# VectorE makes the constants; the first two visits score in banks 0 to 3; first layers of tiles 0 and 1 by w_in piece and half tile; the written orders are replaced

## The chip, the core and the metric

One NeuronCore of a Trainium2 chip runs the whole program. The metric is the device time of one execution in microseconds (us). The core has TensorE (PE, matrix products into PSUM), VectorE (DVE), ScalarE (ACT), GpSimd (POOL) and SyncE (SP). In this kernel POOL issues all input loads, SP issues the stores and the transposing copies. PSUM has eight banks; the kernel numbers them 0 to 7, and the names at0, at1 (two banks each, later la0 to la3) are banks 0 to 3, mp0 to mp3 banks 4 to 7.

## The reference: what is computed

Sliding-window causal attention, then a two-layer feed-forward network with silu on its output:

```python
# q, k, v: 8 batches x 8 heads x 576 positions x 64, float32
scores = (q @ k.T) / sqrt(64)                 # a query sees itself and the 63 keys before it
attn = softmax(where(0 <= i - j < 64, scores, -1e9)) @ v
x = attn.transpose(0, 2, 1, 3).reshape(4608, 512)
h = x @ w_in                                   # w_in 512 x 2048
out = (h * sigmoid(h)) @ w_out                 # w_out 2048 x 512
```

## The kernel before, in words

**Attention.** The 8 x 9 blocks of 64 queries are taken four at a time: 18 visits, u = 0 to 17, each with all 8 heads. A visit has the steps s (scores, 64 small products with 32-row weights, L391 for u below 5, L378 later), exp (two ACT instructions of 1024 columns, L403), mask, pv (32 products with 64-column weights, L431 or L418), inverse and norm on DVE (L442, L445), and the turn of the result into the layout of the network's input: by PE and a copy (ot L457, bridge L464) for visits 0, 1, 2, 3 and 5, by a transposing DMA on SP otherwise. Visits 0 and 1 have no mask step: a product of the identity with a window matrix puts a large negative number into the banks before the scores are added (bias, L386). In visit 1 bias and scores go to banks 4 to 7 (UP = 4), and its four exp instructions take 512 columns each.

**What feeds a visit.** POOL loads the rows of k and q of a visit (L315), DVE transposes them (turn_blocks, L321), and copies of 32 rows move the preceding key block beside each one (shift_k, L308, on ACT or DVE). The values v come in as pairs of blocks (load_v, L338) and are shifted by 64 partitions (shift_v, L362).

**Network.** 4608 tokens are nine tiles of 512. For tiles 0 to 5 the first layer takes 16 column tiles of w_in (ft) by 4 chunks (c): for one ft four products of 512 columns fill one of banks 4 to 7, and ACT takes silu of it (L472, L477). Tile 0's first six ft are computed in two halves of 256 tokens instead (NF0 = 6), so that they can begin when visit 0 alone is done. The second layer of tile 0 is plain (L540), from tile 1 on a seven-product (Strassen) form is used (L544), and tiles 6 to 8 use it in the first layer too (L502). Some products are issued as two halves of 64 weight columns (expert_mm, L467), next to pv, whose weights have 64 columns.

**What sets the order.** Nothing is scheduled by hand in the main part: class Plan (L18) simulates the engines at build time. Every step is added with a class, a duration per engine, its predecessors and, where needed, a group of PSUM banks; within a class steps keep their order, and whenever an engine is free the class head that is ready and has the lowest rank goes next. The ranks are a table of numbers (L237). Loads are one class, in the order of the string SEQ (L166): k and q of visit 0 (letter a), two loads of v, k and q of visit 1 (b), the constants (i), two loads of v, three pieces of w_in (w), a piece of w_out (o), and so on. A piece of w_in is 256 of the 2048 columns. Eight loads at most are under way (L86). PE fills idle time ahead of the first network product with products of zeros ("warm", L974, 41 of them here). A visit's scores may run only after a number of network products (GO, L158).

**Constants.** POOL makes the identity and the window between the loads (L246, L251), ACT copies half of the window (L258), DVE clears the margins of k and v (L265, L269) and makes the 0/1 mask (L261). A silu of a spare tile after the exps of visit 1 brings the table of silu in early (L985).

## Time and profile before

| what | value |
|---|---|
| runs shown | 280.84, 281.28, 280.3 us; median 280.84 us |
| span of the profiled execution (first to last instruction) | 280.6 us |
| mean granted TensorE clock | 0.994 |
| busy | PE 271.8, DVE 203.7, ACT 175.8, POOL 109.3 us |
| first network product | at 19.29 us |
| last PE instruction done | at about 277.1 us |

The span starts 0.24 us ahead of the first instruction that is counted as busy. The profiled execution has no time of its own on record beside its span of 280.6 us; the median of the three runs lies 0.28 us above that span. A timeline row gives start, duration, engine, line, operation, output and input, count, and in brackets how long the engine had been idle and what released it. A window row gives for each engine the busy time (and the number of instructions) in the order PE, PEld (weight loads), DVE, ACT, POOL, then the granted clock, the mean share of DMA engines that are busy, and GB/s.

### The profile page before, as it was taken

The page shows a single profiled execution, that of the slowest core. Times are in us where ns is not written, and L with a number is a line of the kernel's source. Part 1 is how long each engine was busy: PE and PEld are TensorE (multiplying, and loading weights), DVE is VectorE, ACT ScalarE, POOL GpSimd, SP SyncE. Part 2 cuts the span into 40 slices and gives each one's busy share as a digit, 9 for nine tenths or more (in the row PEclk, how much of TensorE's full clock was granted, in tenths as well). Part 3 has the DMA queues.
Part 4 walks back from the last instruction along what each step waited for, and adds up shares of the span by engine and source line. Part 5 has one row for each costly group of instructions (what it writes and reads, how often), then busy time and mean ns, then how long its engine had stood idle before and what let it go on. Part 6 is the DMA issues. An engine that isn't in the chain of part 4 may idle for free.

```text
span 280.6 us, 8735 instructions
## 1 busy us (share of the span) xinstructions
PE 271.8 (97%) x3704; PEld 197.2 (70%) x3704; DVE 203.7 (73%) x380; ACT 175.8 (63%) x272; POOL 109.3 (39%) x163
## 2 busy tenths in 40 slices
PE   8799999999999999899999999999999999999995
PEld 4367445446876488566885488647888888888884
DVE  4682458999868599789698568947587867868641
ACT  2768884976568683857637675665556664565631
POOL 8976776649787599584680000000000000000000
PEclk9979999999999999999999999999999999999999
DMA  9999999999999999999999602540013001101303
GB/s 85 172 197 187 186 185 185 220 220 143 123 217 164 126 146 153 152 177 139 134 165 189 71 2 77 97 96 0 4 37 112 3 32 67 57 0 40 112 20 132
DMA packets 105863, 32.42 MB, mean 116 GB/s; under 512 B 90464, under 2 KB 104800, under 8 KB 105824
## 3 DMA queue, kind: packets, MB, share of 16 engines
q0 software_dynamic: 82336, 19.02, 84.4%
q1 hardware_dynamic: 23488, 12.85, 22.6%
q8 instruction: 29, 0.48, 0.8%
q14 instruction: 10, 0.08, 0.1%
HBM read 38.01 MB, written 9.44 MB: 169 GB/s over the span
## 4 chain that ended last, share of the span: by engine, by line
PE 83%; DMA 8%; issue 3%; DVE 3%; POOL 2%; ACT 1%; DVEq 0%; POOLq 0%; ACTq 0%
PE mp L470 57%; PE la L509 8%; PE la L470 6%; PE mp L509 5%; DMA vv<-in_v_dram 3%; PE at L374 2%; DMA nat<-in_k_dram 2%; PE at L425 2%; DMA nat<-in_q_dram 2%; PE at L437 1%; POOL vv L345 1%; PE at L461 1%; PE mp L974 1%; POOL nat L316 1%; DVE eo L406 1%
## 5 line engine op out<-in xcount | busy, mean ns | idle before, releaser
L470 PE MATMUL mp<-bridge,w_in_sb 128*128 128x512 bf16 (+3 forms) x521 | 86.7, 367 | 0.2 <-ACT gt L478 0.2
L478 ACT ACTIVATE gt<-mp 128x512 bf16<-128x512 f32 (+1 forms) x102 | 56.6, 573 | 22.0 <-PE mp L470 21.2
L470 PEld LDWEIGHTS <-w_in_sb 128*128 128x128 bf16 (+1 forms) x521 | 41.4, 103 | 38.0 <-issue 0.8
L470 PEld LDWEIGHTS <-gs 128*128 128x128 bf16 x512 | 49.4, 98 | 6.0
L403 ACT ACTIVATE eo<-at 128x1024 bf16<-128x1024 f32 x34 | 34.0, 1027 | 14.0 <-PE at L374 12.7
L470 PEld LDWEIGHTS <-gt 128*128 128x128 bf16 (+1 forms) x422 | 34.1, 102 | 9.5 <-issue 0.4
L470 PE MATMUL mp<-ws,gs 128*128 128x256 bf16 x320 | 40.3, 273 | 0.0
L470 PE MATMUL mp<-w_out_sb,gt 128*128 128x256 bf16 (+3 forms) x278 | 38.6, 310 | 0.0
L345 POOL DMA_DIRECT2D vv<-in_v_dram x38 | 33.6, 898 | 3.0 <-DMA w_out_sb<-in_moe_w_out_dram 1.3
L293 POOL DMA_DIRECT2D nat<-in_q_dram x40 | 24.0, 608 | 17.8 <-DMA vv<-in_v_dram 10.0
L406 DVE TENSOR_TENSOR eo<-eo,mask 128x1024 bf16<-128x1024 bf16 x32 | 21.6, 681 | 6.9 <-ACT eo L403 6.7
L293 POOL DMA_DIRECT2D nat<-in_k_dram x40 | 24.2, 617 | 6.1 <-DMA nat<-in_k_dram 3.0
L909 ACT COPY ot<-mp 128x512 f32<-128x512 f32 (+1 forms) x28 | 15.8, 563 | 15.5 <-PE mp L470 14.4
L520 ACT ACTIVATE eo<-vv 128x512 bf16<-128x512 f32 (+1 forms) x18 | 13.9, 773 | 16.2 <-DVE vv L800 16.2
L445 DVE TENSOR_TENSOR eo<-at,rc 128x512 bf16<-128x512 f32 x36 | 22.9, 674 | 0.2
L533 DVE TENSOR_TENSOR gs<-gt 128x1024 bf16<-128x1024 bf16 x24 | 16.3, 686 | 8.5 <-ACT gt L478 8.5
L912 DVE TENSOR_TENSOR ot<-mp,ot 128x512 f32<-128x512 f32 (+1 forms) x21 | 13.8, 658 | 5.7 <-PE mp L470 4.6
L800 DVE TENSOR_TENSOR vv<-mp,vv 128x512 f32<-128x512 f32 x15 | 10.3, 689 | 7.1 <-PE mp L509 7.1
L509 PEld LDWEIGHTS <-w_in_sb 128*128 128x128 bf16 x144 | 14.1, 98 | 1.6
L800 DVE TENSOR_TENSOR vv<-la,vv 128x512 f32<-128x512 f32 x21 | 13.8, 683 | 2.0 <-PE la L509 1.7
L470 PE MATMUL mp<-w_out_sb,gs 128*128 128x256 bf16 x112 | 14.0, 273 | 0.0
L470 PE MATMUL mp<-ws,gt 128*128 128x256 bf16 (+1 forms) x128 | 11.8, 273 | 0.2 <-DVE ot L912 0.2
(121 smaller groups left out, 384.7 us busy)
## 6 DMA issues: line engine op xcount, KB each, us to landing
out_dram<-ot SPq DMA_DIRECT2D x32, 256.0 KB, 3.3
vv<-in_v_dram POOLq DMA_DIRECT2D x38, 128.0 KB, 6.6
nat<-in_k_dram POOLq DMA_DIRECT2D x40, 72.0 KB, 5.8
nat<-in_q_dram POOLq DMA_DIRECT2D x40, 72.0 KB, 5.5
w_in_sb<-in_moe_w_in_dram POOLq DMA_DIRECT2D x8, 256.0 KB, 8.4
w_out_sb<-in_moe_w_out_dram POOLq DMA_DIRECT2D x8, 256.0 KB, 8.1
out_dram<-ot SPq DMA_DIRECT2D x8, 128.0 KB, 1.8
nat<-in_k_dram POOLq DMA_DIRECT2D x3, 256.0 KB, 6.2
```

What stands on the lines that cost most here:

```text
L293: nc.gpsimd.dma_start(out=nats[i].bitcast(BF16)[32 * r:32 * r + 32].rearrange("s (g y) -> s g y", y=128), in_=(q, k)[kk][b, h].rearrange(" ...
L345: nc.gpsimd.dma_start(out=vv[b % NVB][:, t, :, 0:D], in_=v[b, :, 64 * t - 64:64 * t + 64].rearrange("h s d -> s h d"),)
L403: nc.scalar.activation(out=dst, in_=src, func=ACTF.Exp, scale=scale)
L406: nc.vector.tensor_mul(es[w], es[w], mask)
L445: nc.vector.tensor_mul(oxs[o].rearrange("p x c (r d) -> p x (c r) d", r=2), at_pv(op, hf)[:, :, :, 0:D], rcs[r].unsqueeze(3).to_broadcast( ...
L470: nc.tensor.matmul(o[cols], lhsT=w[:, cols], rhs=x, **kw)
L478: nc.scalar.activation(out=gts[0][:, ft, lo:hi], in_=bank(bk)[:, lo:hi], func=ACTF.Silu)
L509: nc.tensor.matmul(bank(bk)[:, HT * f:HT * f + HT], lhsT=w[:, c, 128 * (2 * u + f):128 * (2 * u + f) + 128], rhs=rhs, start=first and f == ...
L520: nc.scalar.activation(out=gt_of(j)[:, f0:f0 + 2, lo:hi], in_=src, func=ACTF.Silu)
L533: (nc.vector.tensor_sub if i else nc.vector.tensor_add)(sums[i][:, f0:f1], x[:, f0:f1], y[:, f0:f1])
L800: d[k] = p.add("plus", {"DVE": 0.69}, lambda _: nc.vector.tensor_add(o, halves(bk), o), [op] + deps)
L909: return p.add("piece", {"ACT": 0.18 + 0.0008 * n}, lambda e: copies[e](out=flat(o), in_=bank(bk)[:, 0:n]), [end] + deps)
```

## The change

- **Constants on DVE.** POOL's five instructions and ACT's copy are replaced by DVE instructions: a row 0 to 127 by doubling (one memset and seven additions), its transpose as a column, three additions of 32, 64 and 96, the identity by comparing row and column, the window from the square of the distance (three instructions), and a copy of half of it. POOL then issues only loads.
- **Visit 1 in banks 0 to 3.** bias is four steps, one for each bank, and exp of visit 1 is two instructions of 1024 columns, as in visit 0.
- **First layers of tiles 0 and 1** in jobs: one piece of w_in (two ft) by half a tile (256 tokens), eight products of 256 columns into one bank, and one silu for both ft. A job needs one piece and one visit's output.
- **Orders.** For every step of visits 0 to 3, the constants and the jobs of both tiles, a written order for each engine (SCRIPT) replaces the ranks; the loads ahead have a written order of 70 (LOADS); new ranks; the gates count PE time (AFTER) in place of products (GO); WHOLE names 19 stretches of products that are not halved. The spare silu is dropped.

The core of the diff (the long tables are cut to a line or two, and durations given to the planner are left out):

```diff
-    def const_ident(_):
-        nc.gpsimd.memset(ident, 0.0)
-        nc.gpsimd.affine_select(out=ident, in_=ident, compare_op=ALU.not_equal, fill=1.0, ...
+    def const_row(n):
+        if n == 0:
+            nc.vector.memset(row[:, 0:1], 0.0)
+        else:
+            nc.vector.tensor_scalar_add(row[:, n:2 * n], row[:, 0:n], float(n))
+    def const_column(_):
+        nc.vector.transpose(out=column, in_=row[:, 0:32])
+    def const_quarter(r):
+        rows = slice(32 * r, 32 * r + 32)
+        nc.vector.tensor_scalar_add(column[rows, 0:1], column[rows, 0:1], 32.0 * r)
+    def const_ident(_):
+        nc.vector.tensor_scalar(ident, row, column[:, 0:1], None, op0=ALU.is_equal)
+    def const_far(_):
+        nc.vector.tensor_scalar(far, row[:, 0:64], column[:, 0:1], 32.5, op0=ALU.subtract, op1=ALU.add)
+    def const_away(_):
+        nc.vector.tensor_tensor(out=away, in0=far, in1=far, op=ALU.mult)
     def const_window(_):
-        nc.gpsimd.memset(window, 0.0)
-        nc.gpsimd.affine_select(...)
-        nc.gpsimd.affine_select(...)
+        nc.vector.tensor_scalar(window, away, 1024.0, -32768.0, op0=ALU.is_gt, op1=ALU.mult)
     def const_window0(_):
-        nc.scalar.copy(out=window0[64:128], in_=window[64:128])
+        nc.vector.tensor_copy(out=window0[64:128], in_=window[64:128])
...
-    def bias(u):
-        for r in range(4):
-            nc.tensor.matmul(bank_at(UP * u + r), lhsT=ident, ...
+    def bias(u, r):
+        nc.tensor.matmul(bank_at(r), lhsT=ident, ...
     def scores_blocks(u):
-                    o = bank_at(r + (UP if u == 1 else 0))
+                    o = bank_at(r)
...
+    def first_early(op, j, f, h):
+        v0 = 4 * j % NBR + 2 * h
+        for s in range(2):
+            for c in range(NDC):
+                ft = 2 * f + s
+                nc.tensor.matmul(bank(op)[:, HT * s:HT * s + HT], lhsT=w_in_sb[:, c, ft * 128:(ft + 1) * 128],
+                                 rhs=bridge[:, v0:v0 + 2, c], start=(s == 0 and c == 0), stop=(s == 1 and c == NDC - 1),
+                                 skip_group_check=True)
+    def silu_early(bk, f, h):
+        nc.scalar.activation(out=gts[0][:, 2 * f:2 * f + 2, HT * h:HT * h + HT], in_=halves(bk), func=ACTF.Silu)
...
-    p.add("prime", {"ACT": 0.2}, lambda _: nc.scalar.activation(out=spare, in_=zero, func=ACTF.Silu), ...
-            si = (add_first_seven if seven else add_first)(n_tile, pool)
+            si = (add_first_seven if seven else add_first if n_tile > 1 else add_first_early)(n_tile, pool)
-    SEQ = "a v b i v w w w o w w w y w o w c d o o v y o o e o o y".split()
+    SEQ = "a v b v w w w o w w w y w o w c d o o v y o o e o o y".split()
+    LOADS = [0, 1, 4, 3, 2, 6, 7, 5, 17, 14, 10, 8, 13, 19, 9, 20, 22, 21, 23, 28, 12, 24, 11, 27, 18, 26, 15, 25, 16, ...
+        "PE": ( "bias3 bias2 bias0 bias1 s0 pv0 pv1 bias6 ot0 bias7 bias4 ot1 bias5 s1 job6 job5 pv2 pv3 job2 job0 ot3 ot2 job4 job10 "
+            "job8 job7 job9 job13 job14 job12 job15 job3 job1 job11 s2 s3 pv4 ot5 pv5 ot4 ot6 ot7 job20 job16 ...
```

Job n is piece n of w_in with visit 0's tokens for n below 8, and piece n - 8 with visit 1's tokens for 8 to 15.

How the instructions move, at three places. First DVE from the end of the clearing of margins to the turn of visit 0's q. Names: kt holds visit 0's keys, qt its queries, nat a loaded tile; gs is lent to visit 1's keys. Before:

```order
L266 MEMSET vv_84 128x72
L267 MEMSET vv_84 64x8x32
L275 MEMSET window_68 128x64
L276 MEMSET zero 128x4
L958 MEMSET kt_81 32x8x64
L322 STREAM_TRANSPOSE kt_81<-nat_70 128x8x2x32
L313 COPY kt_81<-kt_81 32x8x128
L322 STREAM_TRANSPOSE qt_79<-nat_71 128x8x2x32
```

Now, the last rows of the constants and the same steps:

```order
L303 TENSOR_SCALAR far<-row,column 128x64
L306 TENSOR_TENSOR away<-far 128x64
L338 MEMSET window_70 128x64
L309 TENSOR_SCALAR window<-away 128x64
L1028 MEMSET kt_83 32x8x64
L319 MEMSET vv_84 128x72
L320 MEMSET vv_84 64x8x32
L312 COPY window_70<-window 64x64
L382 STREAM_TRANSPOSE kt_83<-nat_72 128x8x2x32
L300 TENSOR_SCALAR ident<-row,column 128x128
L373 COPY kt_83<-kt_83 32x8x128
L382 STREAM_TRANSPOSE qt_81<-nat_73 128x8x2x32
```

Sixteen new DVE instructions now stand ahead of the first turn and the identity stands right behind it; one small memset has gone and one pair that clears a margin of v stands later.

Second, POOL's queue from its first load. Before:

```order
L316 DMA nat_70<-in_k_dram 128x8x128
L316 DMA nat_71<-in_q_dram 128x8x128
L345 DMA vv_82<-in_v_dram 128x8x64 x2
L316 DMA nat_72<-in_k_dram 128x8x128
L316 DMA nat_73<-in_q_dram 128x8x128
L252 MEMSET window 128x64
L253 ISA
L253 AFFINE_SELECT window<-window 128x64
L255 AFFINE_SELECT window<-window 128x64
L247 MEMSET ident 128x128
L248 AFFINE_SELECT ident<-ident 128x128
L345 DMA vv_82<-in_v_dram 128x8x64 x2
```

Now:

```order
L376 DMA nat_72<-in_k_dram 128x8x128
L376 DMA nat_73<-in_q_dram 128x8x128
L376 DMA nat_74<-in_k_dram 128x8x128
L405 DMA vv_84<-in_v_dram 128x8x64 x4
L376 DMA nat_75<-in_q_dram 128x8x128
L411 DMA w_in_sb<-in_moe_w_in_dram 128x4x256 x7
```

The first eight loads are the same eight; visit 1's q moves from the sixth place to the eighth and its k from the fifth to the third. Behind them the row before has three pieces of w_in, one of w_out, three of w_in and two loads of v; now seven pieces of w_in follow at once.

Third, PE where the network begins ("..." for repeated rows). Before, after the turns of visit 0's output:

```order
L461 MATMUL mp_115<-ident,eo 128x128
...
L437 MATMUL at_112<-vv_82,eo 64x65
...
L470 LDWEIGHTS w_in_sb
L470 MATMUL mp_113<-bridge,w_in_sb 64x256
```

Now, from visit 1's scores:

```order
L456 MATMUL at_114<-qt_81,gs_93 128x64
L541 LDWEIGHTS w_in_sb
L541 MATMUL mp_115<-bridge,w_in_sb 128x256
...
L496 MATMUL at_113<-vv_84,eo 64x65
...
L541 MATMUL mp_118<-bridge,w_in_sb 128x256
```

Before, all pv of visit 1 stood ahead of the first network product; now the first two jobs (16 products) stand between visit 1's scores and its pv.

235 lines of the change are left out of this document (133 added, 102 removed), and 13 rows, old and new, of the table SCRIPT.

## The prediction

> **What bounds the kernel now.** The page first: its span and its line of busy time.
>
> ```profile
> span 280.6 us, 8735 instructions
> PE 271.8 (97%) x3704; PEld 197.2 (70%) x3704; DVE 203.7 (73%) x380; ACT 175.8 (63%) x272; POOL 109.3 (39%) x163
> ```
>
> PE is busy for 97% of the span, so only PE's work, PE's waits and what stands ahead of its first useful product count. Next the windows by stage, which tell where PE is not busy (first number after the length).
>
> ```profile
> 10.00:20.00 10.00, 7.66 (x165) 4.92 (x166) 8.03 (x17) 7.61 (x12) 8.48 (x12) 0.83 1.64 189
> 40.00:60.00 20.00, 19.91 (x254) 10.26 (x254) 17.26 (x30) 15.07 (x23) 11.41 (x18) 1.00 1.52 214
> 80.00:100.00 20.00, 19.85 (x321) 12.30 (x319) 15.14 (x30) 15.67 (x23) 14.88 (x23) 1.00 2.10 162
> 100.00:120.00 20.00, 18.80 (x397) 14.59 (x397) 17.30 (x34) 13.29 (x18) 15.53 (x24) 1.00 1.61 153
> 140.00:160.00 20.00, 19.61 (x276) 12.62 (x262) 15.05 (x34) 11.42 (x18) 6.16 (x8) 1.00 1.42 151
> 264.00:281.00 17.00, 13.11 (x121) 11.51 (x118) 6.02 (x12) 5.17 (x13) 0.00 (x0) 1.00 0.24 78
> ```
>
> From 20 us to the last product PE is idle for 0.09 + 0.15 + 1.20 + 0.39 = 1.83 us; the windows not shown there are full, and the last one holds the end, where the stores finish. What else can be gained lies in the opening and at the end. There busy time misleads, since products of zeros count as work; the timeline tells them apart, and the chain of waits gives PE from 19.45 on.
>
> ```profile
> 5.65 0.71 DVE L322 STREAM_TRANSPOSE kt<-nat 128x512 f32<-128x512 f32 x1 [2.08 <-DMA nat<-in_k_dram]
> 9.32 0.68 PE L397 MATMUL at<-qt,kt 32*128 32x64 bf16 x64
> 9.67 1.04 ACT L367 COPY vv<-vv 64x1024 bf16<-64x1024 bf16 x1 [1.75 <-DMA vv<-in_v_dram]
> 10.73 1.02 ACT L403 ACTIVATE eo<-at 128x1024 bf16<-128x1024 f32 x1
> 11.06 0.71 DVE L322 STREAM_TRANSPOSE gs<-nat 128x512 f32<-128x512 f32 x1 [1.12 <-DMA nat<-in_k_dram]
> 14.61 0.67 PE L397 MATMUL mp<-qt,gs 32*128 32x64 bf16 x62 [0.51 <-DVE gs L313]
> 14.82 0.69 DVE L445 TENSOR_TENSOR eo<-at,rc 128x512 bf16<-128x512 f32 x1
> 16.54 0.50 DVE L365 COPY vv<-vv 64x512 bf16<-64x512 bf16 x1
> 17.41 1.28 ACT L985 ACT_TABLE_LOAD   x1
> 18.41 1.04 PE L437 MATMUL at<-vv,eo 128*64 128x65 bf16 x32
> 19.29 1.25 PE L470 MATMUL mp<-bridge,w_in_sb 128*64 128x256 bf16 x20
> ```
> ```profile
> 20.87 0.66 PE mp L470 x6
> 21.75 12.56 PE mp L470 x74
> 34.31 0.62 PE at L397 x58
> 249.17 0.87 PE mp L470 x8
> ```
>
> The first network product starts at 19.29. By 21.75 visits 0 and 1 are finished and 20 half products and 6 whole ones of 256 columns are done, 16 in all; eight of that size take 0.87 us (last row), so 1.74 us of the first layer. From there to the scores of visit 2 at 34.31 PE has no gap. So the figure to beat is 21.75 - 1.74 = 20.01: the time at which an unbroken first layer would have begun, with both visits' attention out of the way.
>
> **The loads.** The loads go through one queue in order. Asked for a single load each, the views of the eighth load (the second of the two of v that take 1.80 us from 8.04, so issued at about 8.9) and of the first piece of w_in (issued at 9.81) give, from issue to landing:
>
> ```profile
> DMA to landing us min/median/max: 5.3/5.6/5.9
> DMA to landing us min/median/max: 5.7/5.7/5.7
> 8.04 1.80 POOL L345 DMA_DIRECT2D vv<-in_v_dram  x2
> 9.81 2.26 POOL L351 DMA_DIRECT2D w_in_sb<-in_moe_w_in_dram  x3
> 19.78 0.77 POOL L351 DMA_DIRECT2D w_in_sb<-in_moe_w_in_dram  x1 [0.58 <-DMA w_out_sb<-in_moe_w_out_dram]
> 21.12 0.60 POOL L316 DMA_DIRECT2D nat<-in_k_dram  x1 [0.57 <-DMA w_in_sb<-in_moe_w_in_dram]
> ```
>
> The eighth load thus lands by 14.8 (8.9 + 5.9) and the ninth by 15.5. POOL waits for pieces of 256 KB landing one after the other, and its two issues are 1.34 us apart: that is the pace of w_in and w_out. The first eight loads are the same eight in the change, in another order. So the eighth, now visit 1's q, lands at about 14.9, and the pieces of w_in at about 15.5, 16.9, 18.2, 19.5, 20.9, 22.2 and 23.5. POOL's constants gone buy nothing here: the queue, not POOL, sets the landings. What DVE's additions beside POOL's first issues do to them no row shows; that is rival 4.
>
> **The change, step by step: the opening.** Prices for small DVE instructions:
>
> ```profile
> L276 DVE MEMSET zero<- 128x4 f32 x1 | 0.1, 62 | 0.0
> L262 DVE TENSOR_SCALAR mask<-window 128x64 bf16<-128x64 bf16 x1 | 0.4, 380 | 0.0
> L442 DVE RECIPROCAL rc<-at 128x8 f32<-128x8 f32 x36 | 6.7, 197 | 3.4 <-PE at L425 2.3 <-PE at L437 0.2
> L267 DVE MEMSET vv<- 64x256 uint32 x3 | 0.8, 272 | 0.0
> L266 DVE MEMSET vv<- 128x72 bf16 x3 | 0.4, 118 | 0.6 <-issue 0.6
> 3.08 0.48 DVE L958 MEMSET kt<- 32x512 f32 x1
> ```
>
> - *Constants.* Before, DVE was done with its clearing at 3.56 and waited until 5.65 for visit 0's k: 2.1 us of cover. One memset of 62 ns and one clearing pair leave (118 + 272 ns and 0.2 of idling): 0.65 us, so 2.9. Sixteen instructions come in: at 62 ns each they end near 3.9, at 380 ns near 9.0. Thirteen depend on the one before, like the reciprocal (197 ns), which I take: 13 x 0.2 + 3 x 0.06 = 2.8 us, so DVE is ready at 5.7, just at the landing. The identity, about 0.3, then stands between the two turns.
> - *Visit 0.* The identity no longer waits for POOL; scores come at about 8.1 in place of 9.32, exps follow from 8.9 without the 1.04 copy of v ahead of them on ACT. pv waits for v: the fifth load, which lands where the fifth landed before, near 11.05, and a shift of 0.5. pv then ends near 12.0. On DVE follow two reciprocals, two norms (0.69) and three small copies: second norm done at about 14.5, so visit 0's output can be in place by about 15.
> - *Visit 1.* q lands at 14.9, turn 0.71, scores 0.67: 15.7 to 16.4. Behind the turn on DVE stand a shift of 0.3 and visit 0's second bridge, 0.42, done at 16.4. So the first job starts at **16.5**; its piece landed at 15.5. This is the step on which most rests: 19.29 becomes 16.5.
> - *From there.* Two jobs of 0.87: 18.25. ACT does visit 1's exps from 16.5 to 18.6 (1.02 each), so pv of its second half waits 0.4 and ends at 19.1. Jobs 2 and 0 (pieces landed at 18.2 and 19.5): 20.9. The two turns of visit 1's output, about 0.45, wait for nothing, since its norms end near 20.6: 21.4. Four jobs, 3.5 us of first layer, are done then. Figure to compare: 21.4 - 3.5 = 17.9, against 20.01: **2.1 us earlier**.
> - *Table of silu.* The spare silu's load (1.28) ended in idle time; now it comes after the last exp, 18.6 to 19.9, and the first silu follows at 20.5 and is needed when a fifth job wants a bank, at 21.4. Nothing, with 0.9 to spare; if this cover went, as much as ACT were late.
> - *First layer's rest.* Twelve jobs of 0.87 from 21.4 end at 31.9. At 109 ns for 256 columns they cost what 512 columns cost, and the work of PE is the same otherwise: 384 products of 512 columns in the first layers of tiles 0 to 5, before and after. Halved pairs fall by about a quarter; I set this at 0 (-0.3 to +0.3).
> - *Thin covers.* PE now comes 2 us earlier to loads that come no earlier. At the pace of 1.34 us for 256 KB, and in the new order of loads, w_out's first piece lands at about 30.6 (needed at 31.9), its second at 33.2 (34.3), visit 3's q at 36.6 and is turned at 37.3 (38.7). Each has about 1 us, less where small loads go slower than that pace or DVE is busy; I take 0.4 us off. Bounds: 0 and 2.1, the whole gain.
>
> **The middle.** The waits of 1.83 us are small and single; the largest is this one.
>
> ```profile
> 117.97 0.54 PE L425 MATMUL at<-vv,eo 128*64 128x65 bf16 x22 [1.20 <-issue]
> ```
>
> It lies inside one pv, with nothing in the profile that ended it. The new orders put scores of visits 4, 8, 12 and 15 later by 2 to 14 us of PE work (visit 4 after tile 1's first layer), which takes exps out of the silus' way and gives loads time. I take 0.6 us of the 1.83 away. Bounds: all of it away, or 2 us of new waits, as much as is there now.
>
> **The sum.** 280.6 - 2.1 + 0.4 - 0.6 = 278.3 against the span; runs shown lie 0.28 higher at the median: **278.6 us**, -0.8%. A measurement can tell about 0.3% (0.84 us) from no change.
>
> **Rivals.**
>
> 1. *The clock drops on useful work.* The rows are these:
>
> ```profile
> 12.43:15.84 3.41, 1.44 (x84) 1.25 (x85) 3.25 (x7) 2.15 (x4) 3.29 (x5) 1.00 1.60 192
> 15.84:19.26 3.42, 3.42 (x45) 1.97 (x44) 2.74 (x7) 3.04 (x6) 2.55 (x4) 0.50 1.37 199
> 114.80:118.20 3.40, 2.20 (x42) 1.27 (x40) 2.37 (x5) 3.37 (x5) 1.16 (x3) 1.00 1.41 129
> ```
>
> After 3.41 us with 1.44 busy the granted clock is 0.50 for the next 3.42; a stretch with 2.20 busy of 3.40 is not followed by one. Before, that slow stretch covered fillers and pv and ended at 19.26, just as the network began. Now 16.5 to 19.26 is useful. If it is slow again, products of about 2.7 us take twice as long, less the 0.4 of waiting that this swallows and half of it regained while pieces are awaited: about 1.4 us lost, 280.0. Against it: between 12.4 and 15.8 PE now has pv's end, five fillers (0.8), four bias products and two turns (1.3) and part of scores, some 2.4 us. Chance 0.13. By the Trainium skill, page TensorE: Matmul & The Clock Gate, Part 1, the windows are 3.4 us long, run freely, and the clock falls after an idle one. The trace agrees on the length (3.41 us), but a window that was 42% busy was enough.
>
> 2. *Slower: DVE's constants are late.* Each microsecond by which the first turn is late moves visit 0's chain, and behind its norms the turn of visit 1's q; the cover is 0.4 us (14.5 against 14.9). At the 380 ns of the row, DVE is ready at 9.0, 3.3 late; the first job starts 2.9 late, PE idles meanwhile and its clock drops (1.4): 278.6 + 2.9 + 1.4 = 282.9. It decides from 2.5 us of lateness on. For it: the only such instruction in the trace took 380 ns. Against: that row began while a turn was still running. Chance 0.11.
>
> 3. *The gain is given back.* Earlier work meets loads that are no earlier (thin covers), or a new order of DVE and ACT makes waits in the middle: 2.1 + 0.6 lost, 280.8. Chance 0.15.
>
> 4. *Descriptors.* If DVE's constants hold POOL's first load by 1 us (about the length of one issue), all landings and with them the first job move by that: 279.6. Chance 0.06. For it: DVE and POOL have not worked side by side on such instructions in any row. Against it: the load that POOL issued while DVE copied 32 rows took 0.93 us, no longer than two others (1.80).
>
> ```profile
> 5.70 0.93 POOL L316 DMA_DIRECT2D nat<-in_q_dram  x1
> ```
>
> This rival is what a rule of the Trainium skill would make of the change: its page SBUF — State Buffer, section SBUF: two separate sides, says that a DVE instruction in a two-port mode keeps GpSimd from writing the descriptors of its DMAs. The one overlap above does not show it.
>
> **Numbers.** The forecast has the remaining 0.55, and its own range is 277.0 to 279.7 (thin covers 0 to 1, middle -1.8 to +0.3). Faster by over 0.3%: 0.55, rival 4 and two fifths of rival 1, and a part of 3 (0.04) = 0.70. Same: the rest of 1, most of 3 = 0.18. Slower: 0.12. The range takes in rivals 1, 3 and 4 and leaves out 2: 276.8 to 280.9.
>
> **What would show it.** The first product of the changed first_early at 16.5 (16 to 17.5); the turn of visit 1's q at 14.9, ended by its load; DVE's first turn at 5.65 to 6.2; granted clock 1.00 from 6 to 20; visit 2's scores near 32.3 in place of 34.31; POOL without waits for its own constants. Wrong is the forecast if the first job starts after 18.5, if PE waits over 1 us between 22 and 45, or if idle PE time from 45 to 277 exceeds 3 us.

## The result and the profile after

| | kernel before | kernel after |
|---|---|---|
| median of four runs each, on one chip | 280.86 us (280.3 to 281.28) | 284.3 us (282.44 to 285.21) |
| span of the profiled execution | 280.6 us | 281.7 us (that execution took 283.42 us) |

The ratio after to before is 1.0124, 95% interval [1.0075, 1.0173]: 1.2% slower, where 0.8% faster was forecast, and outside the range. Here and below a ratio leaves out the executions that the chip ran in a slower state, while medians and ranges hold all of them. The medians lie 3.4 us apart and the two spans only 1.1: before's profiled execution was about 1.5 us longer than its median, as is worked out further down. So either the loss behind the opening is larger than this pair of traces gives, or the gain ahead of it is smaller.

The page of after, span and busy time:

```profile
span 281.7 us, 8757 instructions
PE 273.3 (97%) x3750; PEld 206.0 (73%) x3750; DVE 204.6 (73%) x399; ACT 170.6 (61%) x259; POOL 109.1 (39%) x158
```

The opening, from the timeline of after (start, duration, engine, line, operation):

```profile
1.12 2.03 DVE L290 TENSOR_SCALAR row<-row 128x1 f32<-128x1 f32 x7
4.52 0.38 DVE L303 TENSOR_SCALAR far<-row,column 128x64 f32<-128x64 f32 x1
6.74 0.71 DVE L382 STREAM_TRANSPOSE kt<-nat 128x512 f32<-128x512 f32 x1
8.97 0.68 PE L456 MATMUL at<-qt,kt 32*128 32x64 bf16 x64
15.06 0.71 DVE L382 STREAM_TRANSPOSE qt<-nat 128x512 f32<-128x512 f32 x1
```

And from the chain that ended last in after, the pieces of the opening:

```profile
16.57 1.91 PE mp L541 x16
19.11 1.85 PE mp L541 x16
21.41 10.48 PE mp L541 x96
32.32 0.62 PE at L456 x56
```

The first job starts at 16.57 (forecast 16.5), the first layer runs unbroken from 21.41 (forecast 21.4), and the scores of visit 2 stand at 32.32 (forecast 32.3; before 34.31). The opening does what was forecast: visit 2's scores come 1.99 us earlier. From there to the end of the span before needs 280.6 - 34.3 = 246.3 us and after 281.7 - 32.3 = 249.4 us. So **3.1 us are lost behind the opening**, and the windows of after show where:

```profile
10.00:20.00 10.00, 9.10 (x181) 6.34 (x180) 7.55 (x18) 6.25 (x8) 6.72 (x10) 1.00 1.67 188
20.00:40.00 20.00, 20.00 (x276) 14.63 (x276) 8.25 (x19) 14.82 (x25) 13.95 (x19) 1.00 1.63 189
40.00:60.00 20.00, 20.00 (x235) 14.80 (x229) 17.37 (x32) 11.12 (x18) 11.07 (x17) 1.00 1.42 202
60.00:80.00 20.00, 18.79 (x413) 15.81 (x411) 17.53 (x33) 12.36 (x19) 19.54 (x30) 1.00 1.78 147
80.00:100.00 20.00, 19.42 (x250) 11.50 (x248) 15.29 (x31) 14.59 (x22) 15.51 (x24) 1.00 1.89 185
100.00:120.00 20.00, 19.81 (x464) 14.88 (x465) 18.48 (x37) 14.67 (x19) 18.93 (x28) 1.00 1.80 159
120.00:140.00 20.00, 19.41 (x238) 12.97 (x238) 12.40 (x25) 10.42 (x17) 12.38 (x20) 1.00 1.64 156
```

PE is full to 60 us, then idle for 1.21 + 0.58 + 0.19 + 0.59 us up to 140. A window counts a stretched product as busy, so the idle time understates the loss. A finer measure, used below and in the expectations, is the time from the start of one product to the start of the next beyond the usual for its shape, wherever that is over 0.06 us; these are called PE's waits. From 45 to 130 us they come to 2.05 us before (1.36 of it the stop inside one pv at 116.8) and to 4.56 us after; behind 130 us to 0.73 and 1.17. Together that is 2.95 us more, nearly all of the 3.1.

The two largest places of after, first around 63 us. Rows of POOL, of DVE and of PE, in brackets the idle time ahead and what ended it:

```profile
54.66 1.20 POOL L353 DMA_DIRECT2D nat<-in_q_dram  x2 [6.03 <-DVE qt L382]
56.75 0.58 POOL L346 DMA_DIRECT2D nat<-in_q_dram  x1
62.13 1.26 DVE L392 STREAM_TRANSPOSE qt<-nat 128x576 f32<-128x576 f32 x1 [2.83 <-DMA nat<-in_q_dram]
63.23 0.68 DVE L604 TENSOR_TENSOR gs<-gt 128x1024 bf16<-128x1024 bf16 x1
67.37 0.83 PE L529 MATMUL mp<-ws,gs 128*128 128x256 bf16 x6 [0.92 <-DVE gs L604]
```

GpSimd's queue stood 6.03 us on a batch 3 query load whose buffer came free only when VectorE had turned visit 4's q. Batch 2's last query load stood behind it, was issued at 56.75 and landed at 62.1. VectorE's order had its turn ahead of tile 1's sums, so VectorE stood 2.83 us, the sums began at 63.23, and PE waited for them at 66.4. The second place is 117 to 124 us:

```profile
117.71 0.78 DVE L395 STREAM_TRANSPOSE kt<-nat 128x576 f32<-128x576 f32 x1 [0.88 <-DMA nat<-in_k_dram]
118.62 1.29 DVE L504 TENSOR_TENSOR eo<-at,rc 128x512 bf16<-128x512 f32 x2
120.53 0.78 DVE L395 STREAM_TRANSPOSE qt<-nat 128x576 f32<-128x576 f32 x1 [0.63 <-DMA nat<-in_q_dram]
122.23 1.29 DVE L504 TENSOR_TENSOR eo<-at,rc 128x512 bf16<-128x512 f32 x2
122.97 0.44 PE L484 MATMUL at<-vv,eo 128*64 128x65 bf16 x16 [0.41 <-DVE eo L504]
```

Two turns that wait for loads stand ahead of two visits' norms (L504), and the next pv waits for those norms.

### The profile page after: what moved, and what is told of

It reads as the page before. It is cut to its first block, busy times and chain, and to the rows that moved or that the text cites. A ratio compares the mean times of both kernels' runs of the same rounds, so it can differ in the third digit from the quotient of the medians.

```text
span 281.7 us, 8757 instructions
## 1 busy us (share of the span) xinstructions
PE 273.3 (97%) x3750; PEld 206.0 (73%) x3750; DVE 204.6 (73%) x399; ACT 170.6 (61%) x259; POOL 109.1 (39%) x158
## 4 chain that ended last, share of the span: by engine, by line
PE 66%; DMA 14%; DVE 9%; POOL 8%; issue 3%; ACT 0%; DVEq 0%; POOLq 0%
PE mp L529 37%; PE la L580 8%; DMA nat<-in_k_dram 8%; PE la L529 6%; PE mp L541 5%; POOL nat L353 5%; PE mp L580 5%; DMA vv<-in_v_dram 4%; DMA nat<-in_q_dram 2%; POOL vv L405 2%; PE at L484 1%; PE at L434 1%; DVE eo L465 1%; DVE qt L395 1%; DVE eo L504 1%
## 5 line engine op out<-in xcount | busy, mean ns | idle before, releaser
L529 PE MATMUL mp<-bridge,w_in_sb 128*128 128x512 bf16 (+1 forms) x336 | 58.2, 379 | 0.4 <-ACT gt L549 0.4
L529 PEld LDWEIGHTS <-gs 128*128 128x128 bf16 (+1 forms) x529 | 49.4, 99 | 7.2 <-DVE gs L604 1.5
L549 ACT ACTIVATE gt<-mp 128x512 bf16<-128x512 f32 x64 | 36.8, 599 | 17.0 <-PE mp L529 16.9
L462 ACT ACTIVATE eo<-at 128x1024 bf16<-128x1024 f32 x36 | 35.5, 1024 | 16.1 <-PE at L434 11.2
L529 PEld LDWEIGHTS <-w_in_sb 128*128 128x128 bf16 (+1 forms) x336 | 26.2, 104 | 26.0 <-issue 0.9
L529 PE MATMUL mp<-ws,gs 128*128 128x256 bf16 (+1 forms) x328 | 40.3, 273 | 0.9 <-DVE gs L604 0.9
L529 PE MATMUL mp<-w_out_sb,gt 128*128 128x256 bf16 (+2 forms) x264 | 37.7, 309 | 0.0
L405 POOL DMA_DIRECT2D vv<-in_v_dram x38 | 34.3, 920 | 3.2 <-DMA nat<-in_k_dram 1.5
L541 PE MATMUL mp<-bridge,w_in_sb 128*128 128x256 bf16 x256 | 28.7, 273 | 0.1
L541 PEld LDWEIGHTS <-w_in_sb 128*128 128x128 bf16 x256 | 24.8, 98 | 3.2
L465 DVE TENSOR_TENSOR eo<-eo,mask 128x1024 bf16<-128x1024 bf16 x32 | 21.4, 672 | 5.0 <-ACT eo L462 4.8
L504 DVE TENSOR_TENSOR eo<-at,rc 128x512 bf16<-128x512 f32 x36 | 23.1, 682 | 0.2
L546 ACT ACTIVATE gt<-mp 128x512 bf16<-128x512 f32 x32 | 17.3, 597 | 4.1 <-PE mp L541 3.9
L580 PEld LDWEIGHTS <-w_in_sb 128*128 128x128 bf16 x144 | 14.1, 98 | 2.4 <-issue 0.8
```

Source lines behind the costliest of these rows:

```text
L405: nc.gpsimd.dma_start(out=vv[b % NVB][:, t, :, 0:D], in_=v[b, :, 64 * t - 64:64 * t + 64].rearrange("h s d -> s h d"),)
L462: nc.scalar.activation(out=dst, in_=src, func=ACTF.Exp, scale=scale)
L465: nc.vector.tensor_mul(es[w], es[w], mask)
L504: nc.vector.tensor_mul(oxs[o].rearrange("p x c (r d) -> p x (c r) d", r=2), at_pv(op, hf)[:, :, :, 0:D], rcs[r].unsqueeze(3).to_broadcast( ...
L529: nc.tensor.matmul(o[cols], lhsT=w[:, cols], rhs=x, **kw)
L541: nc.tensor.matmul(bank(op)[:, HT * s:HT * s + HT], lhsT=w_in_sb[:, c, ft * 128:(ft + 1) * 128], rhs=bridge[:, v0:v0 + 2, c], start=(s == ...
```

## The experiments

Sixteen kernels. Ratios are to the kernel before, run beside each on the same chip. The letters k, q, v name loads; names such as turn13 are the planner's: class and number within the class. A turn is VectorE's transpose of loaded keys or queries (turn13 is batch 2's last query turn), a shift its copy of loaded values, a sum an addition for the seven-product form, and dma a load. "Network work" is PE time of the network's products alone, at 0.216 us for 512 columns.

### 1. One table at a time put back

Theories: the new order of the loads, or the new ranks, make the middle slow; or the opening itself.

```diff
 e1_loads_in_order
-    LOADS = [0, 1, 4, 3, ..., 36, 38, 33, 34, 44, 39, 52, ...]
+    LOADS = [0, 1, 4, 3, ..., 36, 38, 33, 34, 35, 39, 40, 41, ...]
 e2_q4_together
-    LOADS = [..., 30, 36, 38, 33, 34, 44, 39, 52, 42, 35, ...]
+    LOADS = [..., 30, 36, 35, 38, 33, 34, 44, 39, 52, 42, ...]
 e3_old_ranks
-    RANK, AFTER, WHOLE: the new tables
+    RANK, AFTER, WHOLE: as before (AFTER in us of network work)
 e4_both_old: the edits of e1_loads_in_order and e3_old_ranks
```

> The changed kernel with the written order of loads kept for the first 36 and the remaining 34 back in the order of the code; nothing else is edited, though the planner then orders the later steps anew around it. Theory A (the queue of loads: in the changed kernel POOL stands still for 6.03 us from 48.6 on behind a load of batch 3 whose buffer is freed by visit 4's q, and the loads run after PE until 124 us): POOL's longest stop falls under 3 us, PE's waits between 45 and 130 fall from about 5 us to under 2.5, time 279.5 to 282. Theory B (the new ranks and gates make the waits, through DVE and ACT): waits stay, time 283 to 285. Theory C (the opening costs what it seems to gain): 283 to 285 as well.

> The changed kernel with one load moved: the second half of visit 4's q directly behind its first half, seven places earlier, so that its buffer is free before batch 3 wants it. Theory A in its narrow form (this one place blocks the queue): POOL's stop of 6.03 us falls under 2.5 us and the time to 280 to 282.5. Theory A in its wide form (loads of batches 2 and 3 are mixed all along): half of that, 282 to 284. Theories B and C: 283 to 285.

> The changed kernel with the ranks, the gates (the old counts of products turned into PE time) and the halving of all stretches of the kernel before; written orders of the opening and of the loads stay. Theory B: PE's waits between 45 and 130 fall under 2.5 us, time 279.5 to 282. Theory A: POOL's stop near 48 us stays at 5 to 7 us and the time at 283 to 286.

> Both edits of e1 and e3 together: only the opening (constants, banks, jobs, written orders, the first 36 loads) is that of the change. If the opening gains what its trace shows (visit 2's scores about 2 us earlier than before), the time is 278 to 280, below the kernel before. Theory C: no faster than the kernel before, 281 to 284.

| | median | ratio, interval | PE's waits 45 to 130 us |
|---|---|---|---|
| e1_loads_in_order | 287.85 us | 1.0176 [1.0075, 1.0278] | 5.6 us |
| e2_q4_together | 284.07 us | 1.0106 [1.0070, 1.0143] | 4.8 us |
| e3_old_ranks | 289.48 us | 1.0183 [1.0035, 1.0331] | 6.8 us |
| e4_both_old | 289.26 us | 1.0174 [1.0036, 1.0311] | 8.6 us (clock 0.96 in this stretch, so not comparable) |

None goes back to the time before; all keep the gain of the opening to about 50 us and lose it by 125. No single table is the cause. The long stop of GpSimd alone is not it either: without it (e1_loads_in_order) PE's waits are 5.6 us, and shortened to 3.4 us (e2_q4_together) 4.8. e4_both_old missed both of its expectations; it is slower than either. On this chip before alone spread from 279.9 to 286.5 us, so no order among the four is read from it. With a table changed the planner orders everything anew, so such a kernel never differs in one thing alone. The largest waits named are new ones each time, and of the kind seen above; e1_loads_in_order has GpSimd's long stop gone and stops of 0.87 and 1.23 us on VectorE, of which this is the second:

```profile
118.69 0.78 DVE L394 STREAM_TRANSPOSE kt<-nat 128x576 f32<-128x576 f32 x1 [1.23 <-DMA nat<-in_k_dram]
```

### 2. Visit 4 earlier, tile 1 whole, and before's order behind the new opening

Visit 4's scores moved from 50.9 us before to 63.5 us after, behind tile 1's whole first layer. Two kernels bring them forward. The third replaces the planner's choice by lists: each engine runs the instructions that it is told, one by one.

```diff
 e5_visit4_early
-    LOADS = [..., 38, 33, 34, 44, 39, 52, 42, 35, ...]      ACT: "... shift11 ... silu18 kshift16 silu21 ..."
+    LOADS = [..., 38, 33, 34, 36, 35, 44, 39, 52, 42, ...]  ACT: "silu20 silu24 kshift16 silu16 ..."
-    AFTER = [12.69, 10.59, 31.72, ...
+    AFTER = [12.69, 10.59, 14.0, ...
 e8_tile1_whole
-            si = (... add_first if n_tile > 1 else add_first_early)(n_tile, pool)
+            si = (... add_first if n_tile else add_first_early)(n_tile, pool)
 e6_frozen (with the line above)
+        for e, names in FROZEN.items():
+            self.queues[e] = [every.pop(name) for name in names.split()]
```

> Visit 4's q is loaded right behind batch 2's last k and q, its key shift stands nine silus earlier in ScalarE's written order, and its scores may run from 14.0 of network work, so that PE computes them at 42 us of work and not at 51 (before: 37). If the late visit 4 is what squeezes visits 4 to 7 and eats the lead, PE's waits between 45 and 130 us fall from after's 4.6 us to 2.5 or less and the time is 2 us or more below after's, ratio to the kernel before 1.003 or less. If the orders of the middle as a whole are the cause, or the feed is, the waits move to other places and stay at 4 to 6 us, ratio 1.008 to 1.018.

> The new opening (constants on VectorE, banks 0 to 3, tile 0's first layer by piece and half tile, the first 36 loads of the new order), and from tile 0's second layer on PE, VectorE, ScalarE and SP each run the instructions of the kernel before in its own order, one by one; loads behind the first 36 in code order. If the new orders behind the opening lose what it gains, this keeps the lead: first job at 16.5, PE's waits between 45 and 130 us near before's 2.0 us, span 278 to 279.5, ratio to the kernel before 0.990 to 0.997. If loads or VectorE feed the middle at a pace that an earlier PE only waits for, the lead of 2 us is gone by 60 us of network work (91.4 us, as before), the waits between 45 and 130 us are 4 us or more, ratio 0.998 to 1.003. If the opening itself leaves something behind that costs later, ratio 1.008 or more, as in the four kernels that had it so far.

> The kernel after, with tile 1's first layer by whole tile and in the scheduler's order (its 16 jobs and silus leave the written orders); only tile 0's stays by w_in piece and half tile. Visit 4's scores come at 41 us of work, visit 5's at 47. If the written order of tile 1 is the cause, PE's waits between 45 and 130 us are 2.5 us or less and the ratio to the kernel before is 1.003 or less. If the new ranks, loads and bounds of the visits are, they stay at 4 us or more and the ratio is 1.008 or more.

e5_visit4_early took 288.96 us (ratio 1.0300 [1.0283, 1.0318]), with 10.3 us of waits; e8_tile1_whole 290.82 us (1.0351 [1.0322, 1.0379]), with 12.1 us. Both are worse than after. Bringing visit 4 forward among the other new tables made more waits than it took away, so its late place by itself is not shown to be the cause. e6_frozen took 294.08 us (1.0474 [1.0456, 1.0493]), and its profile shows a stop at the seam of the two orders, which says nothing on either order but much on the mechanism. Waits of PE, and VectorE's timeline:

```profile
PE mp L656 <- ACT gt L661: 11.9, 1, 11.9
```
```profile
38.86 0.42 DVE L542 COPY vv<-vv 64x1024 bf16<-64x1024 bf16 x1 [14.93 <-DMA vv<-in_v_dram]
39.87 0.71 DVE L497 STREAM_TRANSPOSE kt<-nat 128x512 f32<-128x512 f32 x1
```

The new load order brings this value load long after before's VectorE order comes to it. VectorE stood on it for 14.93 us; visit 2's key turn stood behind it; a key shift on ScalarE waited for that turn, silus stood behind the shift, and PE got no bank for 11.9 us. Behind the seam, from 60 to 130 us, PE's waits are 1.9 us, about as before (1.8).

### 3. The four corners: old or new opening, old or new middle

e9_frozen mends the seam; e10_frozen_loads has all 70 loads in the new order as well; e11_old_opening is the kernel before up to the end of tile 0's first layer and then the kernel after's own order.

```diff
 e9_frozen
     FROZEN["DVE"]: the new order up to mask2, then before's     FROZEN["ACT"]: the new order up to kshift11, then before's
     FROZEN["PE"]: the new order up to job11, then before's
 e10_frozen_loads
-    FROZEN["POOL"]: "... dma36 dma38 dma33 dma34 dma35 dma39 dma40 ..."
+    FROZEN["POOL"]: "... dma36 dma38 dma33 dma34 dma44 dma39 dma52 ..."
 e11_old_opening
     the code before, with add_first_early for tile 1; FROZEN: before's order up to moe87, kshift13, kshift11, then after's
```

> As the last frozen kernel, but VectorE and ScalarE keep the new order up to visit 2's third mask and visit 3's key shifts, so that neither stands behind a value load that lands later than before; from there on all engines run before's own order, and loads behind the first 36 go in code order. If the new orders of the middle lose what the opening gains: scores of visit 4 at 49, PE's waits between 45 and 130 us of 2.5 us or less, ratio to the kernel before 0.990 to 0.997. If loads or VectorE feed the middle at a pace that an earlier PE only waits for: level with before at 61 us of network work, 4 us or more of waits, ratio 0.998 to 1.003. If the opening leaves something that costs later whatever the order: ratio 1.008 or more.

> The same orders of PE, VectorE, ScalarE and SP, with all 70 loads in the new order. If the new load order behind the opening costs by itself (visit 4's q at 45 us, and GpSimd's queue standing behind a load whose buffer is not free), this is 1 us or more above the kernel with code order, with waits of PE on the turned keys and queries of visit 4 and batch 3 behind 50 us; if not, the two are within 0.3%.

> The other corner: the kernel before through tile 0's first layer (constants on GpSimd, banks as before, loads in code order), and from there on the kernel after's own order on PE, VectorE, ScalarE and SP, one by one, tile 1's first layer by piece and half tile included. If the middle's orders cost 2 to 4 us by themselves: visit 2's scores at 34.5, PE's waits between 45 and 130 us 4 us or more, ratio to the kernel before 1.010 to 1.020. If the middle costs only because PE comes to it earlier (a feed), PE reaches 61 us of network work at 91.4 to 92 us and the ratio is 0.998 to 1.004.

| | median | ratio, interval | waits 22 to 60 us | waits 60 to 130 us |
|---|---|---|---|---|
| before: old opening, old middle | | 1 | 0.3 us | 1.8 us (1.36) |
| after: new, new | 284.3 us | 1.0124 [1.0075, 1.0173] | 0.1 us | 4.5 us (0.20) |
| e11_old_opening: old, new | 286.54 us | 1.0187 [1.0137, 1.0236] | 2.2 us | 4.7 us (0.29) |
| e9_frozen: new, old | 284.31 us | 1.0111 [1.0073, 1.0149] | 5.2 us | 1.6 us (0.84) |
| e10_frozen_loads: new, old, new loads | 288.53 us | 1.0268 [1.0219, 1.0317] | 9.3 us | 1.4 us (0.78) |

In brackets the part of a stop "issue", of which more at the end. From 60 to 130 us the waits go with the middle, not with the opening: 1.4 to 1.9 us with before's order, 4.5 and 4.7 with the new one. The new middle waits as much when PE comes to it late (e11_old_opening), so its waits are not only those of a PE that is early. By its ratio e9_frozen lies where its expectation put a loss that the opening leaves behind; in its trace that loss stands ahead of 60 us.

The corner of new opening and old middle is not a clean one. e9_frozen waits 5.2 us ahead of 60, more than the 2 us by which PE is early, since what PE waits for lands later than before: visit 3's queries at 37.90 us (35.05 before) and a load of values at 44.27 (39.80 before). The new order of the first 36 loads, which is kept here, puts pieces of w_out ahead of both. VectorE in e9_frozen, with the norms that PE waits for in the last row:

```profile
37.92 0.71 DVE L497 STREAM_TRANSPOSE qt<-nat 128x512 f32<-128x512 f32 x1 [3.67 <-DMA nat<-in_q_dram]
44.30 0.69 DVE L542 COPY vv<-vv 64x1024 bf16<-64x1024 bf16 x1 [2.25 <-DMA vv<-in_v_dram]
45.87 1.29 DVE L619 TENSOR_TENSOR eo<-at,rc 128x512 bf16<-128x512 f32 x2
```

So it is again an order of loads that does not fit the order of the steps. And since the kernels with before's middle reach 60 us late, how that middle does with a PE that is 2 us early is not shown.

The largest waits of e10_frozen_loads and the stop behind them, waits of PE and timeline of VectorE:

```profile
PE at L635 <- DVE eo L619: 6.2, 2, 3.7
```
```profile
51.99 0.71 DVE L497 STREAM_TRANSPOSE qt<-nat 128x512 f32<-128x512 f32 x1 [3.42 <-DMA nat<-in_q_dram]
53.50 1.29 DVE L619 TENSOR_TENSOR eo<-at,rc 128x512 bf16<-128x512 f32 x2
```

Again a turn that stands on its load, with a norm behind it. In e9_frozen, with the loads behind the 36th in code order, the same turn is at 48.66, and PE's wait of 3.8 us at 50.4 is one of 0.2: the most part of 4.4 us of span (286.1 against 281.7) is the place of one query load. And e11_old_opening, with after's VectorE order, shows the place of 117 to 124 us in large. Timeline of VectorE, then of PE:

```profile
123.61 0.78 DVE L457 STREAM_TRANSPOSE qt<-nat 128x576 f32<-128x576 f32 x1 [2.85 <-DMA nat<-in_q_dram]
```
```profile
126.05 0.44 PE L547 MATMUL at<-vv,eo 128*64 128x65 bf16 x16 [2.63 <-DVE eo L567]
```

### 4. VectorE's late steps moved behind what PE waits for

So the theory became: VectorE runs its list in order; where the list has a step that reads a load ahead of sums, masks or norms, and the load lands later than the planner thought, the whole of VectorE stops, and PE with it. The test takes the kernel after, instruction for instruction on all engines, and moves single steps; for e13_old_opening_turns it takes e11_old_opening.

```diff
 e12_turns_later, e13_old_opening_turns: VectorE's order
   wsum7
-  turn13
   sum0 shift12 sum1 shift13 sum2 sum3
+  turn13
   sum4 shift14 sum5 ...
   shift27
-  turn28
   inverse18 inverse19 norm18 norm19
-  turn29
+  turn28
   mask19 inverse20 inverse21 norm20 norm21
+  turn29
   shift28
```

> The kernel after, instruction for instruction on every engine, but for three of VectorE's transposes of loaded keys and queries, put 2 to 8 places later in its order: batch 2's last query turn behind the first half of tile 1's sums, and the two turns of 115 to 121 us behind the norms of visits 9 and 10. If the theory holds that VectorE's in-order queue stands on loads that land late, with the sums and norms that PE waits for behind them, then PE's waits at 66.4 (1.08 us) and between 119 and 124 us (1.35 us) go: PE's waits between 45 and 130 us fall from 4.6 to about 2.2 us, the span from 281.7 to about 279.5, the ratio to the kernel before to 1.000 to 1.005. If the rival holds (VectorE or the loads are short of pace in the middle, and the stall moves elsewhere), the waits stay at 4 us or more and the ratio at 1.009 to 1.016.

> The kernel with before's opening and after's middle, with the same three turns put later on VectorE and nothing else. There PE's wait at 123.3 us (2.8 us) stood behind VectorE's 2.85 us stop for a query load. By the theory of the late loads in VectorE's order it goes, and the span falls from 285.2 to 282 or 282.7; by the rival of a short pace the stall reappears within 15 us, and the span stays at 284.5 or more.

e12_turns_later: 283.06 us, 1.0072 [1.0048, 1.0095]. e13_old_opening_turns: 285.27 us, 1.0152 [1.0122, 1.0183], span 283.3. Both lie between the two expectations, and their intervals overlap those of after and of e11_old_opening, so it is the traces that speak here. The waits of 119 to 124 us are gone in both (1.35 and 2.8 us), and no other took their place before 130. The wait at 66 us did not go; it grew from 1.08 to 1.80 us, and the timeline of VectorE says why, with PE's row behind it:

```profile
62.77 0.91 DVE L540 COPY vv<-vv 64x1024 bf16<-64x1024 bf16 x1 [0.66 <-DMA vv<-in_v_dram]
65.97 1.25 DVE L505 STREAM_TRANSPOSE qt<-nat 128x576 f32<-128x576 f32 x1
67.07 0.68 DVE L717 TENSOR_TENSOR gs<-gt 128x1024 bf16<-128x1024 bf16 x1
```
```profile
67.80 1.81 PE L642 MATMUL mp<-ws,gs 128*128 128x256 bf16 x15 [1.63 <-DVE gs L717]
```

The next step in the list was late too (a value copy), and the turn now stood ahead of the fifth sum, which PE needs. A new wait of 1.2 us came at 149 us, behind another value copy that stood 1.02 us on its load.

```diff
 e14_loads_behind: VectorE's order, on top of turn28 and turn29 above
-  turn13 sum0 shift12 sum1 shift13 sum2 sum3 sum4 shift14 sum5 mask4 sum6 sum7
+  sum0 sum1 sum2 sum3 sum4 sum5 turn13 mask4 sum6 sum7 shift12 shift13 shift14
-  mask25 shift34 inverse24 inverse25 norm24 norm25
+  mask25 inverse24 inverse25 norm24 norm25 shift34
 e15_norms_first: on top of it
-  shift12 shift13 shift14 turn14 mask5 mask6 shift15 mask7 inverse8 inverse9 norm8 norm9
+  shift12 shift13 mask5 shift14 mask6 turn14 inverse8 inverse9 norm8 norm9 shift15 mask7
-  sum43 plus7 plus8
+  plus7 plus8 sum43
```

> The kernel after, instruction for instruction, but for VectorE's order: the three turns put later as before (batch 2's last query turn now behind the sixth sum), and also the three value copies of batch 2 that stood between tile 1's sums (behind all eight sums) and one value copy at 148.8 us (behind visit 12's norms). If late loads in VectorE's order are the rest of the loss, PE's waits at 66.1 (1.80 us) and 149.4 (1.18 us) of the last kernel fall below 0.5 us each, the span from 281.4 to 278.5 or 279.2, and the ratio to the kernel before to 0.993 to 1.000. If the middle is short of pace by itself, PE waits elsewhere between 66 and 90 us for the same 2 us, and the ratio stays at 1.004 to 1.010.

> The last kernel (all loads-bound steps behind) and, on VectorE alone, five more steps in another place: visit 4's second mask ahead of one value copy, its norms ahead of visit 5's second mask and of two turns of batch 3, and one sum of the product stage behind two additions that PE waits for at 233.5 us. If PE's waits at 71.6, 74.5, 75.4 and 77.6 us (1.98 us together) are made by what stands ahead of masks and norms in VectorE's order, 1.0 to 1.6 us of them go, with 0.3 to 0.5 at 233.5 us; the span falls from 280.4 to 278.5 or 279.2 and the ratio to the kernel before to 0.994 to 0.999. If VectorE is short of pace there (it is busy from 61 to 82 us without a gap), the waits only change their names: 1.7 us or more stay between 66 and 90 us, ratio 1.001 to 1.005.

e14_loads_behind: 282.31 us, 1.0034 [1.0007, 1.0061]. The waits at 66 and 149 us are gone; part came back at 71 to 78 us (1.98 us), where a mask and a norm were late because VectorE now had hardly a gap from 61 to 82 us. So its numbers lie between the two expectations. e15_norms_first: 282.11 us, 1.0042 [1.0020, 1.0065]: no gain. The waits of 71 to 78 us changed their names, as the rival said; the largest of them is now

```profile
PE at L597 <- DVE vv L540: 0.7, 1, 0.7
```

With VectorE full, moving one step ahead makes another late. What should help is work that begins earlier. VectorE had idled 2.4 us just ahead of 61.6, where its next step, a sum, waited for a silu; the turn and the copies that could fill this gap read loads that stood behind GpSimd's stop.

```diff
 e16_no_stop: on top of e14_loads_behind, GpSimd's and VectorE's order
-  dma43 dma40 dma49 dma63 dma54 dma46 dma45 dma56 dma41 dma62
+  dma43 dma40 dma49 dma45 dma46 dma41 dma54 dma63 dma56 dma62
-  wsum7 sum0 ... sum5 turn13 mask4 sum6 sum7 shift12 shift13 shift14
+  wsum7 turn13 shift12 shift13 sum0 ... sum5 mask4 sum6 sum7 shift14
 e17_norms_and_stop: on top of it, VectorE's order
-  shift14 turn14 mask5 mask6 shift15 mask7 inverse8 inverse9 norm8 norm9 turn15 turn16
+  shift14 mask5 shift15 mask6 inverse8 inverse9 norm8 norm9 mask7 turn14 turn15
   inverse10 inverse11 norm10 norm11
+  turn16
   ...
-  turn26 turn27 mask18 shift26 shift27 inverse18 inverse19 norm18 norm19 turn28
+  turn26 mask18 shift26 shift27 inverse18 inverse19 norm18 norm19 turn27 turn28
```

(Both have the move of sum43 as well.)

> On top of the kernel with the loads-bound steps behind: on GpSimd's queue, batch 2's last query load and two of its value loads go ahead of the batch 3 query load whose buffer is free only after visit 4's query turn (there the queue stood 6.0 us, 48.6 to 54.7 us), so that they land by about 56 us and not at 62 to 64; on VectorE the turn and two copies that read them go into its idle 2.4 us before tile 1's sums, and one sum of the product stage behind two additions. By the theory that late loads and the order they force make the loss, VectorE is 2 us ahead from 62 us on, PE's waits of 71 to 78 us (1.98 us) fall to 0.7 us or less, the span goes from 280.4 to 278 or 279, the ratio to the kernel before to 0.992 to 0.998. By the theory that VectorE is short of pace from 62 to 82 us, 1.5 us or more of these waits stay and the ratio is 1.001 to 1.005.

> On top of the last kernel, on VectorE alone: visit 4's norms ahead of visit 5's second mask and of batch 3's turns, and the query turn of 115.4 us (which stood 1.0 us on its load) behind visit 9's norms. The last kernel's new waits of PE were 1.16 us at 80.6 us (tile 2's first layer on the transposing store of visit 4's outputs, issued at 73.5 us, landed at 81.6 us) and 0.74 us at 119.1 us. If they are again made by the order, both fall below 0.4 us, the span is 277.5 to 279, and the ratio to the kernel before 0.992 to 0.998. If the middle's pace is the limit, 1.5 us or more comes back between 66 and 125 us, and the ratio stays within 0.998 to 1.003.

e16_no_stop: 281.13 us, 1.0004 [0.9974, 1.0035], between its two expectations; the interval overlaps that of e14_loads_behind. Rows of GpSimd and of VectorE:

```profile
50.54 0.58 POOL L459 DMA_DIRECT2D nat<-in_q_dram  x1 [1.96 <-DVE bridge L636]
59.23 1.24 DVE L505 STREAM_TRANSPOSE qt<-nat 128x576 f32<-128x576 f32 x1
61.70 0.69 DVE L717 TENSOR_TENSOR gs<-gt 128x1024 bf16<-128x1024 bf16 x1
```

Batch 2's last query load is issued 6.2 us earlier than after's (50.54 against 56.75), its turn fills VectorE's gap, and the waits of 71 to 78 us fall from 1.98 to 0.57 us. Two new ones came in this execution, which took 282.34 us, 1.2 over the median: 0.74 us at 119 us, and one at 80.6 us, where tile 2's first layer reached visit 4's outputs, which the transposing copies had not yet landed:

```profile
PE mp L642 <- DMA bridge<-eo: 1.0, 1, 1.0
```

e17_norms_and_stop: 280.74 us (280.39 to 281.70, 12 runs), 0.9981 [0.9953, 1.0008], where its two expectations meet; both waits are gone, and a wait of 0.79 us for an output copy stands at 78.6. Its page, and the two largest of PE's waits (the first is the wait of PE's fillers at the start):

```profile
span 278.9 us, 8758 instructions
```
```profile
PE mp L1155 <- DVE row L401: 1.1, 1, 1.1
PE mp L642 <- DVE ot L1095: 0.7, 1, 0.7
```

From the kernel after to this one nothing is changed but the places of some twenty steps on VectorE and of five loads on GpSimd, and the ratio went from 1.0124 to 0.9981. The two intervals do not meet: it beats the kernel after, by about 4 us, and that is the sum of the moves; most single ones are too small to be told from no change by their times. Against the kernel before its interval still holds 1, so it is no proven gain.

## Why the prediction was wrong

**The step that failed is the middle**: "I take 0.6 us of the 1.83 away. Bounds: all of it away, or 2 us of new waits." Between the two profiled executions it measured 3.1 us lost in place of 0.6 gained, outside its own bounds. The reason given, that later scores give loads time, was not tested against where the loads stand in the queues. What the runs put in its place: the new lists of GpSimd and VectorE hold loads, and steps that read them, ahead of work that PE needs, and the loads land later than the lists assume. For the two places the traces show it by moves of steps alone: at 119 to 124 us (e12_turns_later, e13_old_opening_turns) and at 66 to 78 us (e14_loads_behind, e16_no_stop). In time it is shown for all moves together, 1.0124 to 0.9981. The rival, that VectorE is short of pace, holds in part: from 61 to 82 us moves within its own list gained nothing (e15_norms_first).

The whole miss, from 278.6 to 284.3 us, adds up so: 3.7 us from the middle, 0.1 from the opening, less the 0.4 of thin covers that did not come, make the span 281.7 in place of 278.3; the sum's base (below) adds 1.4, and after's median lies 0.9 above its profiled execution. The range was also too narrow by its own terms: it let the middle lose only 0.3 us where the text has a bound of 2, and the terms in its bracket add up to 280.1 and not to 279.7.

**Point by point.**

- *Constants.* Forecast 0.2 us for each of 13 dependent instructions and VectorE ready at 5.7; the first turn began at 6.74. So they were 1.1 us late, and visit 0's scores 0.9 late (8.97 against 8.1). The price was right for most of them: five of the seven additions took 0.15 to 0.18 us. The other two took 0.49 and 0.48 us, and each ends where GpSimd ends the issue of a load:

```profile
1.72 0.49 DVE L290 TENSOR_SCALAR row<-row 128x8 f32<-128x8 f32 x1
1.23 1.01 POOL L376 DMA_DIRECT2D nat<-in_k_dram  x1 [0.79 <-POOLq L1105]
2.24 0.90 POOL L376 DMA_DIRECT2D nat<-in_q_dram  x1
```

  The subtraction (0.38 us) and the comparison that makes the window (0.58 us) end so too. At an estimated 0.2 us each, from the other additions, these four would have been about 1.1 us shorter, which is the lateness. What the forecast left out is that such an instruction takes longer when one of GpSimd's issues ends within it (last section). The 380 ns of the mask row, which it weighed as a price, were such a case. The cover held: visit 1's q was turned at 15.06 against 14.9.
- *First job, first layer, visit 2.* 16.57, 21.41 and 32.32 against 16.5, 21.4 and 32.3. Right, and by the mechanism named: one job needs one piece and half a tile.
- *Thin covers.* Forecast 0.4 us; PE is full from 20 to 60 us, so nothing.
- *The sum's base.* The forecast set 0.28 us between span and time. In every execution with both on record it is 1.7 to 1.9 us (after: 283.42 against 281.7). So the profiled execution of before would have taken about 282.3 us, 1.5 more than the median; in the executions behind the later ratios the span of before runs from 278.1 to 282.1 us. With all steps right the forecast would have been 278.3 + 1.7 = 280.0 us, close to before's median.
- *The stop of 1.20 us.* The hope that it goes seems right: at the place that is taken for the same (last section) after stops 0.20 us. That would be 1 us of gain that the middle had, and lost with the rest. It came with the new lists, and not by the reason given.
- *Rival 1, the clock.* Granted 1.00 from 10 to 20 us. It did not come.
- *Rival 2, late constants.* They were late, by 1.1 us, and below the 2.5 us from which the rival decided.
- *Rival 3, the gain is given back.* This is what happened, by the second of its two mechanisms, and it was priced as a gain of 2.7 us lost. The waits were not bounded by the gain: they ate the gain and 1.2% more. In hindsight its chance of 0.15 was small for a kernel in which the lists of all engines were replaced.
- *Rival 4, descriptors.* GpSimd's first two issues took 1.01 and 0.90 us beside VectorE's additions, the same as before's first two. The rule of the Trainium skill named there (page SBUF — State Buffer, section SBUF: two separate sides) is not seen in these rows: GpSimd was not held. It was VectorE's instructions that were lengthened, the other way round from the rival.
- *The marks.* "If idle PE time from 45 to 277 exceeds 3 us" was the mark nearest to the step, but by idle time it was not passed: 2.94 us after (1.84 before). PE's waits, 4.56 us and another 1.17 behind 130 us, against 2.78 before, would have told.

**What stays open.** The opening gains 2.0 us between the two traces, and even the last kernel does not show it against the median of the kernel before. Where before's profiled execution has its 1.5 us over that median is not known. The last kernel's waits from 60 to 130 us are 2.5 us (2.2 without the stop "issue"); before's are 0.4 without it. Before's own middle behind the new opening was run only with the new order of the first loads, and waits 5.2 us ahead of 60 us. Whether some order keeps both was not found.

## What to carry to other kernels

A new list for an in-order engine is a bet on when each load lands. Before pricing it, go down the list of the engine that feeds the bound one, mark each step that reads a load, and ask what stands behind it if the load is 1 to 3 us late; do the same for a load queue whose next buffer is not free. A gain ahead of a middle stage is worth only what the middle's slack lets through, so price the middle with waits that are not bounded by the gain. And set the sum against a time and a span of the same execution.
